# Heads 16 to 31 first in the recurrent-memory step, and the tail projections dealt to four places

## The chip, the core and the metric

The kernel runs on one core of one Trainium2 chip. The metric is the device time in microseconds of one execution; the lower, the better. In the profile the engines are PE (TensorE, matmuls), PEld (its weight loads), DVE (VectorE), ACT (ScalarE), POOL (GpSimd) and SP (SyncE, which issues most DMAs).

## The reference

Four layers in a row, A B A B, on 2048 tokens of 640 channels in bfloat16, each added to its input. Layer A is a segmented attention with a compressive memory (32 heads of 20), and the change doesn't touch it. Layer B carries eight memory tokens through 64 segments of 32 tokens, with 32 heads of 128:

```python
for s in range(n_seg):                      # 64, one after the other
    h = concatenate([mem, xs], axis=1)      # 8 memory tokens, 32 tokens
    q, k, v = h @ Wq, h @ Wk, h @ Wv        # 32 heads of 128 each
    scores = q k^T * scale                  # 40 x 40 a head
    p = softmax(where(mask, scores, -1e9))
    o = (p v) @ Wo
    mem = o[:, :M]                          # the next segment's memory
    outs.append(o[:, M:])
```

The order of the steps is forced: segment s+1 needs the memory that segment s wrote.

## The kernel before

`layer_B` (a loop over `s` from line 914 on) does one segment per step. Two things are worked ahead so that a step has only what depends on the memory. The first is the **tails**: the last 8 tokens of each segment are projected for eight segments at once. `tail_unit(T, k, ...)` (line 757) makes one of eight units of the q and k tails: 8 heads by 5 chunks of 128 channels, 40 matmuls of 64 columns into the PSUM tile `b_tail`; `tail_evac` (772) copies it to `b_tu` and stores that to the DRAM tensor `QKd`; `tails_load` brings a segment's part back as `b_tl`, and POOL copies it into `KT` and `QZ`. `vtail_unit` and `vtail_evac` do the same for v. Each step does one unit of the following group of segments. The second is the state of a step: the projections in step `s` (`b_Ka`, `b_Qa`, `b_Kb`, `b_Qb`, `b_Va`, `b_Vb`; a is heads 0 to 15, b heads 16 to 31) are of the 8 memory tokens of segment s and of 24 tokens of segment s+1, 32 columns together. So half of a transposed tile goes to this step's `KT[s]`, `QT[s]` (the DVE `scatter`), and the other to the next step's (`x_scatter` on ACT).

Each projection (`thin_mm`, 714) is 5 chunks of four matmuls, each on 32 columns of the array (rows say 128x512). `kq` (932) scales and casts the result to `b_kq`; `transp4` turns it with four 128x128 transposes (`b_TPak` and so on). The scores live in PSUM tiles called `b_SP`, which start from a mask (`mask_mm`, a 128x128 matmul with the identity). There are 12 groups of 40 columns: groups 0 to 3 hold the tails' scores (`QZ`), 4 to 7 those of heads 0 to 15, 8 to 11 those of heads 16 to 31. Before, groups 0 to 7 share one tile and 8 to 11 have another. Then follow `soft_max`, `soft_sub`, `soft_exp`, `soft_sum`, the reciprocal and `soft_p`, which writes `b_Px` (DVE) and `b_Pm` (POOL); the transposed probabilities `b_PTP`, copied to `b_PTa` and `b_PTb`; the products with v (`pv`, tiles `b_OTP`, copied to `b_OTsb`); the output projection (`b_OPS`, and `b_OPSd` for the deferred rows); the next memory (`b_msb`, `b_MT`, copied into `b_HX`); and `x_out`, two adds on DVE.

On PE, ACT, DVE and POOL the order within a step is exactly the order in which the code is written: every call goes through `_OrdEng` (87), which ties each instruction to the one before it on its engine. SP is not tied (line 28). Small PSUM tiles come in turn from five buffers (`ps_tile`, 629); `b_tail`, `b_OPS` and `b_OPSd` have one each, and `b_TPbq` used that of `b_tail`.

The part of the step that the change rearranges is written like this before:

```python
Ka; ka = kq(Ka, "act");  Qa; qa = kq(Qa, "dve")      # 1005 on
Kb; kb = kq(Kb, "act");  Qb; qb = kq(Qb, "act")
TPak, scatter, x_scatter; TPaq, ...; TPbk, ...
SPa = mask_mm(0); TPbq, ...; SPb = mask_mm(1)
scores((SPa, SPb))                 # a, tails, b
softmax of both, Px, Pm;  Va;  Vb
tail_unit(.., 0, 6)                # 30 matmuls
p_transp(0); p_transp(1)
tail_unit(.., 6, 8); tail_evac     # 10 matmuls
```

Of the kernel before, what the change touches and what calls it, by code (L numbers as in the profile page):

```python
# [18 lines left out]
F32 = mybir.dt.float32  # L19
BF16 = mybir.dt.bfloat16  # L20
ACT = mybir.ActivationFunctionType
ALU = mybir.AluOpType
AX = mybir.AxisListType
# [6 lines left out]
NCH = 5  # L30
# [568 lines left out]
def layer_B(nc, tc, C, W, x_src, xb_src, x_dst, mem0, B_Wv, B_Wo, nsteps=64, out_bf16=False, tag=""):  # L599
    SCB = 1.0 / math.sqrt(128.0)  # L600
    nc_raw = nc
    nc = _OrdNC(tc, nc_raw, engines=ORDER_ENGINES)
    NG = nsteps // 4
    NT = nsteps // 8
    QKd = tc.dram_tile([nsteps, 128, 512], BF16, name=f"b_QKd{tag}")
    VTd = tc.dram_tile([nsteps, 8, 4096], BF16, name=f"b_VTd{tag}")
    with ExitStack() as ctx:
# [21 lines left out]
        def ps_tile(shape, dtype, name):  # L629
            return pp.tile(shape, dtype, name=name, tag="ps")  # L630
# [80 lines left out]
                return HXz[:, :, 0, :]  # L711
            return HX[u // 4][:, :, u % 4, :]

        def thin_mm(cols_ap, Wt, b, name):
            ps = ps_tile([128, 512], F32, name)
            for c in range(NCH):
                for j in range(4):
                    n = 4 * b + j
                    nc.tensor.matmul(ps[32 * j:32 * j + 32, :], lhsT=cols_ap[:, c, :], rhs=Wt[:, c, 512 * n:512 * n + 512],
                                     start=(c == 0), stop=(c == NCH - 1), tile_position=(0, 32 * j), skip_group_check=True)  # L720
            return ps

        def transp4(sb, name, tp=None):
            if tp is None:
                tp = ps_tile([128, 4, 128], BF16, name)
            for i in range(4):
                nc.tensor.transpose(tp[:, i, :], sb[:, 128 * i:128 * i + 128], C.identb[:])
            return tp

        def scatter(eng, tp, b, dst_t, t0, t1, c0):  # L730
            src = tp[:].rearrange("p i (j t) -> p i j t", j=4)[:, :, :, t0:t1]
            dst = dst_t[:, 16 * b:16 * b + 16, c0:c0 + (t1 - t0)].rearrange("p (j i) c -> p i j c", j=4)
            evac(eng, dst, src)
# [20 lines left out]

        tail_ps = {}

        def tail_unit(T, k, i0, i1, shared=False):
            proj, hg = divmod(k, 4)
            Wt = W.wk if proj else W.wq
            if i0 == 0:  # L760
                if shared:
                    tail_ps[0] = ps_tile([128, 8, 64], F32, "b_tail")
                else:
                    tail_ps[0] = po.tile([128, 8, 64], F32, name="b_tail", tag="tail")
            ps = tail_ps[0]
            for i in range(i0, i1):
                h = 8 * hg + i
                for c in range(NCH):
                    nc.tensor.matmul(ps[:, i, :], lhsT=Wt[:, c, 128 * h:128 * h + 128], rhs=TX[T][:, c, :, :].rearrange("p s t -> p (s t)"),
                                     start=(c == 0), stop=(c == NCH - 1))  # L770

        def tail_evac(T, k, eng, home=None):
            proj, hg = divmod(k, 4)
# [52 lines left out]
            for c in range(NCH):  # L826
                nc.sync.dma_start(HX[0][:, c, 1, 0:8], mem0[:, 128 * c:128 * c + 128].rearrange("t p -> p t"))
        for k in range(8):
            tail_unit(0, k, 0, 8, shared=True)
            tail_evac(0, k, "act" if k % 2 == 0 else "dve", (kqp, "kq"))  # L830
            if k % 4 == 1 and 2 + k // 4 < n0:
                ln_norm(2 + k // 4)
            if k % 4 == 3 and 2 + k // 4 < n0:
                ln_spread(ln_ready.pop(0))
# [21 lines left out]
            evac("act" if b == 0 else "dve", Vth[:, b, :], ps[:])  # L856
        vtails_in(0)
        if NT > 1:
            tail_unit(1, 0, 0, 8, shared=True)
            tail_evac(1, 0, "act")  # L860
            vtail_evac(1, 0, vtail_unit(1, 0), "dve")

# [51 lines left out]
        for s in range(nsteps):  # L914
# [13 lines left out]
            def x_scatter(tp, b, D_):  # L928
                if not last:
                    scatter("act", tp, b, D_[s + 1], 8, 32, 8 if D_ is KT else 0)  # L930

            def kq(ps, eng, scale=None):
                sb = kqp.tile([128, 512], BF16, name="b_kq", tag="kq")
                evac(eng, sb[:], ps[:], scale)
                return sb

            GR = ((0, 8), (8, 12))

            def mask_mm(a):
                g0, g1 = GR[a]  # L940
                SP = ps_tile([128, g1 - g0, 40], F32, f"b_SP{a}")
                nc.tensor.matmul(SP[:].rearrange("p g k -> p (g k)"), lhsT=C.identb[:], rhs=mask12[:, g0:g1, :].rearrange("p g k -> p (g k)"),
                                 start=True, stop=False, skip_group_check=True)
                return SP

            def scores(SPs):
                for b in range(2):
                    for j in range(4):
                        for i in range(4):
                            h = 16 * b + 4 * j + i  # L950
                            nc.tensor.matmul(SPs[b][32 * i:32 * i + 32, j + 4 * (1 - b), :], lhsT=QT[s][:, h, :], rhs=KT[s][:, h, :],
                                             start=False, stop=True, tile_position=(0, 32 * i), skip_group_check=True)
                    if b == 0:
                        qz = QZ[s % 2][:].rearrange("p x c -> p (x c)")
                        for j in range(4):
                            for e in range(2):
                                for t4 in range(4):
                                    pr = 8 * (t4 // 2) + 2 * j + t4 % 2
                                    nc.tensor.matmul(SPs[0][32 * t4:32 * t4 + 16, j, :], lhsT=qz[:, 24 * pr + 8 * e:24 * pr + 8 * e + 16],
                                                     rhs=KT[s][:, 2 * pr + e, :],  # L960
                                                     start=False, stop=True, tile_position=(0, 32 * t4), skip_group_check=True)

            negmax = sm.tile([128, 12], F32, name="b_negmax", tag="negmax")
            ssum = sm.tile([128, 12], F32, name="b_ssum", tag="ssum")
            rs = sm.tile([128, 12], F32, name="b_rs", tag="rs")
            E_ = wk.tile([128, 12, 40], BF16, name="b_E", tag="E0")

            def soft_max(a, SP):
                nc.vector.tensor_reduce(out=negmax[:, slice(*GR[a])], in_=SP[:], axis=AX.X, op=ALU.max, negate=True)

            def soft_sub(a, SP):
                n_ = GR[a][1] - GR[a][0]
                nc.vector.tensor_tensor(out=SP[:], in0=SP[:], in1=negmax[:, slice(*GR[a])].unsqueeze(2).to_broadcast([128, n_, 40]), op=ALU.add)

            def soft_exp(a, SP):
                nc.scalar.activation(out=E_[:, slice(*GR[a]), :], in_=SP[:], func=ACT.Exp)

            def soft_sum(a):
                nc.vector.tensor_reduce(out=ssum[:, slice(*GR[a])], in_=E_[:, slice(*GR[a]), :], axis=AX.X, op=ALU.add)

            def soft_p(eng, P_, k0, k1, g0, g1):
                eng.tensor_tensor(out=P_[:, g0:g1, 0:k1 - k0], in0=E_[:, g0:g1, k0:k1],
# [19 lines left out]
                                             tile_position=(32 * j, 0), skip_group_check=True)  # L1002


            Ka = thin_mm(cols, W.wk, 0, "b_Ka")
            ka = kq(Ka, "act")
            Qa = thin_mm(cols, W.wq, 0, "b_Qa")
            qa = kq(Qa, "dve", SCB)
            Kb = thin_mm(cols, W.wk, 1, "b_Kb")
            kb = kq(Kb, "act")  # L1010
            Qb = thin_mm(cols, W.wq, 1, "b_Qb")
            qb = kq(Qb, "act", SCB)

            TPak = transp4(ka, "b_TPak")
            scatter("dve", TPak, 0, KT[s], 0, 8, 32)
            x_scatter(TPak, 0, KT)
            TPaq = transp4(qa, "b_TPaq")
            scatter("dve", TPaq, 0, QT[s], 0, 8, 24)
            x_scatter(TPaq, 0, QT)
            TPbk = transp4(kb, "b_TPbk")  # L1020
            scatter("dve", TPbk, 1, KT[s], 0, 8, 32)
            x_scatter(TPbk, 1, KT)
            SPa = mask_mm(0)
            TPbq = transp4(qb, "b_TPbq", po.tile([128, 4, 128], BF16, name="b_TPbq", tag="tail"))
            scatter("dve", TPbq, 1, QT[s], 0, 8, 24)
            x_scatter(TPbq, 1, QT)
            SPb = mask_mm(1)
            scores((SPa, SPb))
            soft_max(0, SPa)
            soft_max(1, SPb)  # L1030
            soft_sub(0, SPa)
            soft_exp(0, SPa)
            soft_sub(1, SPb)
            soft_exp(1, SPb)
            soft_sum(0)
            soft_sum(1)
            nc.vector.reciprocal(out=rs[:], in_=ssum[:])
            soft_p(nc.vector, Px, 0, 32, 0, 8)
            soft_p(nc.gpsimd, Pm, 32, 40, 0, 12)
# [9 lines left out]
            if ln_ready:  # L1049
                ln_spread(ln_ready.pop(0))  # L1050
            if work:
                tail_unit(work[0], work[1], 0, 6)
            ptpa = p_transp(0)
            PTa = wk.tile([128, 2, 4, 40], BF16, name="b_PTa", tag="PTa")
            ptpb = p_transp(1)
# [2 lines left out]
                for pt, ptp, eng in ((PTa, ptpa, "act"), (PTb, ptpb, "dve")):  # L1058
                    evac(eng, pt[:, :, 2 * hf:2 * hf + 2, :], ptp[:, :, 2 * hf:2 * hf + 2, :])
            if work:  # L1060
                tail_unit(work[0], work[1], 6, 8)
            if unit:
                tail_evac(unit[0], unit[1], "act")
            otf = [ps_tile([128, 2, 4, 40] if j else [128, 4, 40], F32, "b_OTP") for j in range(4)]
            ots = {j: (otf[j][:, 0, :, :], otf[j][:, 1, :, :]) for j in (1, 2, 3)}
# [25 lines left out]
            def vtail_some(n_):  # L1091
                nonlocal vps, vc
                if work and vc < NCH:
                    vps = vtail_unit(work[0], work[1], vc, min(NCH, vc + n_), vps)
                    vc = min(NCH, vc + n_)

            vtail_some(2)
            if not last:
# [5 lines left out]
                for pi, (ca, cb) in enumerate(parts):  # L1104
# [6 lines left out]
                    nc.vector.tensor_copy(dst[:, ca:cb, 0:8], mt[:])  # L1111
                    vtail_some((1, 1, NCH)[pi])
            vtail_some(NCH)
            if unit:
                vtail_evac(unit[0], unit[1], vps, "act")
            if od and od["n"] == 4:
# [111 lines left out]
```

## Time and profile before

| | |
|---|---|
| median of 3 runs | 2793.08 us (2786.16 to 2794.82) |
| the profiled execution's own time | 2787.25 us |
| its span, first to last instruction | 2785.5 us |
| mean granted clock of PE | 0.981 |
| PE busy | 2574.7 us, 92% |
| DVE, ACT, POOL busy | 1686.6, 1584.9, 715.2 us |
| steps of layer B, start to start | 126, sum 1890.7 us, median 14.88 us |

A line of the timeline gives the start in us from the beginning of the span, the duration, the engine, the source line, the operation, what it writes and reads, and how many were merged; in brackets the idle time of the engine before it and what ended that. Nearly all instructions of layer B carry line L101, that of the helper which keeps the order, so they are told apart by their tiles. Matmuls overlap: the duration of a group holds the time in which the last result runs out, and what a group costs PE is the distance from its start to the start of the next. A row of the stretches gives the length, the busy time of PE, PEld, DVE, ACT and POOL with their instructions in brackets, and then the granted clock, the share of the DMA engines and the GB/s.

### The profile page before, as it was taken

The page shows a single profiled execution, that of the slowest core. Times are in us where ns is not written, and L with a number is a line of the kernel's source. Part 1 is how long each engine was busy: PE and PEld are TensorE (multiplying, and loading weights), DVE is VectorE, ACT ScalarE, POOL GpSimd, SP SyncE. Part 2 cuts the span into 40 slices and gives each one's busy share as a digit, 9 for nine tenths or more (in the row PEclk, how much of TensorE's full clock was granted, in tenths as well). Part 3 has the DMA queues.
Part 4 walks back from the last instruction along what each step waited for, and adds up shares of the span by engine and source line. Part 5 has one row for each costly group of instructions (what it writes and reads, how often), then busy time and mean ns, then how long its engine had stood idle before and what let it go on. Part 6 is the DMA issues. An engine that isn't in the chain of part 4 may idle for free. (4 is left out here: it accounts for less than half of the span.)

```text
span 2785.5 us, 146956 instructions
## 1 busy us (share of the span) xinstructions
PE 2574.7 (92%) x65414; PEld 1700.1 (61%) x65480; DVE 1686.6 (61%) x4553; ACT 1584.9 (57%) x3708; POOL 715.2 (26%) x1645
## 2 busy tenths in 40 slices
PE   5888879999999999999978888799999999999998
PEld 3555556666666666666645555556666666666665
DVE  6888854555555555555578888445555555555554
ACT  4888854555555555544458888445555455555443
POOL 4666541111111111111146665411111111111110
PEclk9999979999999999999989999899999999999999
DMA  6111162221212212111120111721211121211110
GB/s 239 41 44 40 30 195 69 45 46 41 45 43 45 43 43 45 43 39 30 41 99 28 51 49 37 231 47 39 42 42 40 40 44 40 43 41 38 39 26 20
DMA packets 322300, 156.36 MB, mean 56 GB/s; under 512 B 245760, under 2 KB 310400, under 8 KB 318592
## 3 DMA queue, kind: packets, MB, share of 16 engines
q1 hardware_dynamic: 320224, 136.47, 19.2%
q8 instruction: 512, 8.39, 1.3%
q10 hardware_dynamic: 1440, 10.49, 1.0%
q14 instruction: 124, 1.02, 0.1%
HBM read 95.15 MB, written 51.71 MB: 53 GB/s over the span
## 5 line engine op out<-in xcount | busy, mean ns | idle before, releaser
L101 PEld LDWEIGHTS <-b_HX 128*32 128x32 bf16 x15360 | 430.2, 97 | 341.0 <-issue 14.1
L101 POOL TENSOR_TENSOR b_Pm<-b_E,b_rs 128x96 bf16<-128x96 bf16 x128 | 63.3, 495 | 1443.2 <-ACT b_Vth L101 1094.2
L400 DVE TENSOR_REDUCE a_nm<-a_S 128x2 f32<-128x1024 f32 (+3 forms) x512 | 396.5, 815 | 51.4 <-PE a_T L101 26.6
L442 ACT ACTIVATE a_PT<-a_T 128x1024 bf16<-128x1024 f32 (+1 forms) x384 | 325.4, 889 | 84.9 <-PE a_T L101 50.6
L101 PE MATMUL b_OPS<-b_wo,b_OTsb 128*32 128x320 bf16 x8192 | 308.0, 301 | 10.3 <-issue 8.5
L101 PEld LDWEIGHTS <-b_OTsb 128*32 128x32 bf16 x8192 | 200.5, 97 | 97.0 <-DVE b_OTsb L101 24.1
L101 DVE CAST b_HX<-b_MT 128x8 bf16<-128x8 f32 x372 | 63.7, 172 | 277.5 <-PE b_MT L101 272.2
L444 POOL TENSOR_SCALAR_AFFINE_SELECT a_PT<-a_PT 128x256 bf16<-128x256 bf16 (+1 forms) x384 | 193.5, 520 | 143.2 <-ACT a_PT L442 141.0
L101 ACT CAST b_msb<-b_OPS 128x64 bf16<-128x64 f32 x378 | 69.3, 256 | 237.7 <-PE b_OPS L101 237.7
L101 ACT CAST b_kq<-b_Kb 128x512 bf16<-128x512 f32 x128 | 74.9, 585 | 201.6 <-PE b_Kb L101 201.6
L101 DVE COPY b_KT<-b_TPak 128x128 bf16<-128x128 bf16 x128 | 28.8, 225 | 227.0 <-PE b_TPak L101 227.0
L101 PE MATMUL b_Va<-b_wv,b_HX 128*32 128x512 bf16 x2520 | 160.8, 380 | 0.0
L101 PE MATMUL b_Vb<-b_wv,b_HX 128*32 128x512 bf16 x2520 | 160.1, 379 | 0.0
L101 PEld LDWEIGHTS <-b_kq 128*128 128x128 bf16 x2080 | 116.8, 98 | 68.8 <-ACT b_kq L101 55.6
L101 PE MATMUL b_Ka<-b_wk,b_HX 128*32 128x512 bf16 x2520 | 158.8, 379 | 0.0
L101 DVE TENSOR_SCALAR b_kq<-b_Qa 128x512 bf16<-128x512 f32 x128 | 88.5, 691 | 115.9 <-PE b_Qa L101 112.9
L101 PE MATMUL b_Kb<-b_wk,b_HX 128*32 128x512 bf16 x2520 | 158.6, 379 | 0.0
L101 PE MATMUL b_Qb<-b_wq,b_HX 128*32 128x512 bf16 x2520 | 158.6, 379 | 0.0
L101 PE MATMUL b_Qa<-b_wq,b_HX 128*32 128x512 bf16 x2520 | 158.6, 379 | 0.0
L101 DVE CAST b_OTsb<-b_OTP 128x160 bf16<-128x160 f32 (+1 forms) x384 | 122.3, 374 | 39.6 <-PE b_OTP L101 39.6
L101 PE MATMUL b_vtail<-b_wv,b_TX 128*32 128x256 bf16 x2880 | 137.7, 271 | 6.6 <-issue 3.5
L101 ACT ACTIVATE b_E<-b_SP 128x320 bf16<-128x320 f32 (+1 forms) x256 | 81.1, 368 | 109.0 <-PE b_Va L101 95.3
(195 smaller groups left out, 5764.8 us busy)
## 6 DMA issues: line engine op xcount, KB each, us to landing
b_QKd<-b_tu SPq DMA_DIRECT2D x128, 128.0 KB
b_tl<-b_QKd SPq DMA_DIRECT2D x128, 128.0 KB
b_wv<-in_B_Wv_dram SPq DMA_DIRECT2D x10, 1024.0 KB
b_wo<-in_B_Wo_dram SPq DMA_DIRECT2D x16, 640.0 KB
b_VTd<-b_vt SPq DMA_DIRECT2D x256, 32.0 KB
b_Vth<-b_VTd SPq DMA_DIRECT2D x512, 16.0 KB
b_XO<-xres SPq DMA_DIRECT2D x256, 30.0 KB
b_wk<-in_B_Wk_dram ACTq DMA_DIRECT2D x5, 1024.0 KB
```

The costliest lines, as they stand in the source:

```text
L101: r = f(*a, **k)
L400: nc.vector.tensor_reduce(out=nm[:, qc, 2 * pr:2 * pr + 2], in_=X[:, :, o:o + w_], axis=AX.X, op=ALU.max, negate=True)
L442: nc.scalar.activation(out=PT[:, :, b:b + width], in_=Y[:, :, 0:width], func=ACT.Exp, scale=SC)
L444: nc.gpsimd.affine_select(out=dv, in_=dv, pattern=[[0, 2], [0, diag], [1, 128]], compare_op=ALU.is_ge, fill=0.0, base=0, channel_multiplie ...
```

## The change

The two head halves change places: `b_Qb`, `b_Kb` and `b_Ka` are projected first, heads 16 to 31 are transposed, masked, scored and taken through max and subtraction while `b_Qa` is still being projected (two of its five chunks come before these scores, three after). The evacuation of `b_Qb` moves from ACT to DVE and that of `b_Qa` from DVE to ACT. The tails' scores get a PSUM tile of their own, so there are three masks of 160 columns, and three of each softmax instruction. `b_TPbq` moves to the five shared buffers. The tail unit, which was cut by heads into 30 and 10 matmuls, is cut by matmuls at 5, 8 and 20: five ahead of `b_TPaq`, three after `b_Vb`, twelve after `b_PTP`, and twenty at the end of the step, with its evacuation behind them. The core of the diff:

```diff
+    TCUT = (5, 8, 20)
...
-            GR = ((0, 8), (8, 12))
+            GR = ((0, 4), (4, 8), (8, 12))
...
-            Ka = thin_mm(cols, W.wk, 0, "b_Ka")
-            ka = kq(Ka, "act")
-            Qa = thin_mm(cols, W.wq, 0, "b_Qa")
-            qa = kq(Qa, "dve", SCB)
-            Kb = thin_mm(cols, W.wk, 1, "b_Kb")
-            kb = kq(Kb, "act")
-            Qb = thin_mm(cols, W.wq, 1, "b_Qb")
-            qb = kq(Qb, "act", SCB)
+            Qb = thin_mm(cols, W.wq, 1, "b_Qb")
+            qb = kq(Qb, "dve", SCB)
+            Kb = thin_mm(cols, W.wk, 1, "b_Kb")
+            kb = kq(Kb, "act")
+            Ka = thin_mm(cols, W.wk, 0, "b_Ka")
+            ka = kq(Ka, "act")
+            TPbq = transp4(qb, "b_TPbq")
+            scatter("dve", TPbq, 1, QT[s], 0, 8, 24)
+            x_scatter(TPbq, 1, QT)
+            TPbk = transp4(kb, "b_TPbk")
+            scatter("dve", TPbk, 1, KT[s], 0, 8, 32)
+            x_scatter(TPbk, 1, KT)
+            SPb = mask_mm(2)
+            Qa = thin_mm(cols, W.wq, 0, "b_Qa", 0, 2)
+            scores(1, SPb)
+            soft_max(8, 12, SPb[:])
+            soft_sub(8, 12, SPb[:])
+            thin_mm(cols, W.wq, 0, "b_Qa", 2, NCH, Qa)
+            qa = kq(Qa, "act", SCB)
             TPak = transp4(ka, "b_TPak")
             scatter("dve", TPak, 0, KT[s], 0, 8, 32)
+            SPt = mask_mm(0)
+            if work:
+                tail_unit(work[0], work[1], 0, TCUT[0])
+            soft_exp(8, 12, SPb[:])
             x_scatter(TPak, 0, KT)
             TPaq = transp4(qa, "b_TPaq")
             scatter("dve", TPaq, 0, QT[s], 0, 8, 24)
             x_scatter(TPaq, 0, QT)
...
+            SPa = mask_mm(1)
+            tail_scores(SPt)
+            scores(0, SPa)
+            soft_max(0, 4, SPt[:])
+            soft_sub(0, 4, SPt[:])
+            soft_exp(0, 4, SPt[:])
+            soft_max(4, 8, SPa[:])
+            soft_sub(4, 8, SPa[:])
+            soft_exp(4, 8, SPa[:])
+            soft_sum(8, 12)
+            soft_sum(0, 4)
+            soft_sum(4, 8)
...
-                tail_unit(work[0], work[1], 0, 6)
+                tail_unit(work[0], work[1], TCUT[0], TCUT[1])
...
-                tail_unit(work[0], work[1], 6, 8)
-            if unit:
+                tail_unit(work[0], work[1], TCUT[1], TCUT[2])
+            if unit and TCUT[2] == 40:
                 tail_evac(unit[0], unit[1], "act")
...
             vtail_some(NCH)
+            if work and TCUT[2] < 40:
+                tail_unit(work[0], work[1], TCUT[2], 40)
+            if unit and TCUT[2] < 40:
+                tail_evac(unit[0], unit[1], "act")
             if unit:
                 vtail_evac(unit[0], unit[1], vps, "act")
```

More of the change, by code (lines that the diff above doesn't have):

```diff
@@ L712, in cols_of, with thin_mm @@
             return HX[u // 4][:, :, u % 4, :]
-        def thin_mm(cols_ap, Wt, b, name):
-            ps = ps_tile([128, 512], F32, name)
-            for c in range(NCH):
+        def thin_mm(cols_ap, Wt, b, name, c0=0, c1=NCH, ps=None):
+            if ps is None:
+                ps = ps_tile([128, 512], F32, name)
+            for c in range(c0, c1):
                 for j in range(4):
@@ L755, in layer_B, with tail_unit @@
         tail_ps = {}
-        def tail_unit(T, k, i0, i1, shared=False):
+        def tail_unit(T, k, n0, n1, shared=False):
             proj, hg = divmod(k, 4)
             Wt = W.wk if proj else W.wq
-            if i0 == 0:
+            if n0 == 0:
                 if shared:
@@ L765, in tail_unit @@
             ps = tail_ps[0]
-            for i in range(i0, i1):
+            for n_ in range(n0, n1):
+                i, c = divmod(n_, NCH)
                 h = 8 * hg + i
-                for c in range(NCH):
-                    nc.tensor.matmul(ps[:, i, :], lhsT=Wt[:, c, 128 * h:128 * h + 128], rhs=TX[T][:, c, :, :].rearrange("p s t -> p (s t)"),
-                                     start=(c == 0), stop=(c == NCH - 1))
+                nc.tensor.matmul(ps[:, i, :], lhsT=Wt[:, c, 128 * h:128 * h + 128], rhs=TX[T][:, c, :, :].rearrange("p s t -> p (s t)"),
+                                 start=(c == 0), stop=(c == NCH - 1), skip_group_check=True)
         def tail_evac(T, k, eng, home=None):
@@ L828, in layer_B @@
         for k in range(8):
-            tail_unit(0, k, 0, 8, shared=True)
+            tail_unit(0, k, 0, 40, shared=True)
             tail_evac(0, k, "act" if k % 2 == 0 else "dve", (kqp, "kq"))
@@ L858, in layer_B @@
         if NT > 1:
-            tail_unit(1, 0, 0, 8, shared=True)
+            tail_unit(1, 0, 0, 40, shared=True)
             tail_evac(1, 0, "act")
@@ L944, in mask_mm, with scores, tail_scores @@
                 return SP
[L946 to L961, printed above, removed]
+            def scores(b, SP):
+                for j in range(4):
+                    for i in range(4):
+                        h = 16 * b + 4 * j + i
+                        nc.tensor.matmul(SP[32 * i:32 * i + 32, j, :], lhsT=QT[s][:, h, :], rhs=KT[s][:, h, :],
+                                         start=False, stop=True, tile_position=(0, 32 * i), skip_group_check=True)
+            def tail_scores(SP):
+                qz = QZ[s % 2][:].rearrange("p x c -> p (x c)")
+                for j in range(4):
+                    for e in range(2):
+                        for t4 in range(4):
+                            pr = 8 * (t4 // 2) + 2 * j + t4 % 2
+                            nc.tensor.matmul(SP[32 * t4:32 * t4 + 16, j, :], lhsT=qz[:, 24 * pr + 8 * e:24 * pr + 8 * e + 16],
+                                             rhs=KT[s][:, 2 * pr + e, :],
+                                             start=False, stop=True, tile_position=(0, 32 * t4), skip_group_check=True)
             negmax = sm.tile([128, 12], F32, name="b_negmax", tag="negmax")
@@ L966, in layer_B, with soft_max, soft_sub, soft_exp @@
             E_ = wk.tile([128, 12, 40], BF16, name="b_E", tag="E0")
[L968 to L979, printed above, removed]
+            def soft_max(g0, g1, SP):
+                nc.vector.tensor_reduce(out=negmax[:, g0:g1], in_=SP, axis=AX.X, op=ALU.max, negate=True)
+            def soft_sub(g0, g1, SP):
+                nc.vector.tensor_tensor(out=SP, in0=SP, in1=negmax[:, g0:g1].unsqueeze(2).to_broadcast([128, g1 - g0, 40]), op=ALU.add)
+            def soft_exp(g0, g1, SP):
+                nc.scalar.activation(out=E_[:, g0:g1, :], in_=SP, func=ACT.Exp)
+            def soft_sum(g0, g1):
+                nc.vector.tensor_reduce(out=ssum[:, g0:g1], in_=E_[:, g0:g1, :], axis=AX.X, op=ALU.add)
             def soft_p(eng, P_, k0, k1, g0, g1):
@@ L1019, in layer_B @@
             x_scatter(TPaq, 0, QT)
[L1020 to L1036, printed above, removed]
+            SPa = mask_mm(1)
[10 more added lines that the diff above has]
+            soft_sum(4, 8)
             nc.vector.reciprocal(out=rs[:], in_=ssum[:])
```

## Prediction

> **What bounds the kernel now.** I read the page first (busy shares), then the waits, then the timeline of single B steps, then the stretches by stage.
>
> ```profile
> PE 2574.7 (92%) x65414; PEld 1700.1 (61%) x65480; DVE 1686.6 (61%) x4553; ACT 1584.9 (57%) x3708; POOL 715.2 (26%) x1645
> ```
>
> TensorE (PE) is busy for 92% of the span, no other engine for more than 61%. The change touches only the 2 x 64 steps of layer B. The starts of the first `b_Ka` matmuls give 126 step lengths: fastest 14.67 us apart from the first of each layer, median 14.88, mean 15.01, 1890.7 in all. One step without pauses, from the timeline (start, duration, engine; 792.74 to 807.41, so 14.67 us):
>
> ```profile
> 795.97 1.25 PE L101 MATMUL b_Qb<-b_wq,b_HX 128*32 128x512 bf16 x20
> ...
> 797.15 0.40 PE L101 MATMUL b_TPak<-c_identb,b_kq 128*128 128x128 bf16 x4
> 797.34 0.60 ACT L101 ACTIVATE b_kq<-b_Qb 128x512 bf16<-128x512 f32 x1 [0.50 <-PE b_Qb L101]
> ...
> 797.99 0.40 PE L101 MATMUL b_TPbq<-c_identb,b_kq 128*128 128x128 bf16 x4
> ...
> 798.22 0.23 PE L101 MATMUL b_SP<-b_mask,c_identb 128*128 128x160 bf16 x1
> ...
> 798.38 0.28 PE L101 MATMUL b_SP<-b_KT,b_QT 128*32 128x40 bf16 x16
> 798.42 0.23 DVE L101 COPY b_QT<-b_TPbq 128x128 bf16<-128x128 bf16 x1 [0.16 <-PE b_TPbq L101]
> 798.50 0.41 PE L101 MATMUL b_SP<-b_KT,b_QZ 128*16 128x40 bf16 x32
> ...
> 798.74 0.32 PE L101 MATMUL b_SP<-b_KT,b_QT 128*32 128x40 bf16 x16
> 798.87 1.28 PE L101 MATMUL b_Va<-b_wv,b_HX 128*32 128x512 bf16 x20
> ...
> 799.01 0.72 DVE L101 TENSOR_REDUCE b_negmax<-b_SP 128x8 f32<-128x320 f32 x2 [0.36 <-PE b_SP L101]
> 799.65 0.72 DVE L101 TENSOR_TENSOR b_SP<-b_SP,b_negmax 128x320 f32<-128x320 f32 x2
> 799.96 1.27 PE L101 MATMUL b_Vb<-b_wv,b_HX 128*32 128x512 bf16 x20
> 800.25 0.63 ACT L101 ACTIVATE b_E<-b_SP 128x320 bf16<-128x320 f32 x2 [0.78 <-PE b_Va L101]
> 800.72 0.71 DVE L101 TENSOR_REDUCE b_ssum<-b_E 128x8 f32<-128x320 bf16 x2 [0.35 <-ACT b_E L101]
> ...
> 801.16 1.05 PE L101 MATMUL b_tail<-b_TX,b_wq 128*128 128x64 bf16 x30
> ...
> 801.47 0.23 DVE L101 RECIPROCAL b_rs<-b_ssum 128x12 f32<-128x12 f32 x1
> 801.73 0.78 DVE L101 TENSOR_TENSOR b_Px<-b_E,b_rs 128x256 bf16<-128x256 bf16 x2
> ...
> 802.22 0.24 PE L101 MATMUL b_PTP<-c_identb,b_Px 128*128 128x128 bf16 x2
> ...
> 802.75 0.45 PE L101 MATMUL b_tail<-b_TX,b_wq 128*128 128x64 bf16 x10
> ...
> 803.13 0.52 PE L101 MATMUL b_OTP<-b_PTa,b_Vth 32*128 32x40 bf16 x32
> ```
>
> PE runs group after group, in program order. A projection of 20 matmuls starts every 1.08 us, five rounds of 0.216. Single starts in the trace put the 64-column tail matmuls 0.029 apart. So the only real hole is before `b_PTP`: 30 tails need 0.87, but 802.22 - 801.16 is 1.06, hence 0.19 of waiting for `b_Px`; the eight `b_PTP` matmuls take 0.53, against 0.42 in steps where the layer-norm transposes fill that hole, hence 0.11 more. **0.30 us a step, 38 us in all, is the most that an earlier softmax can win**, besides the pauses of PE at "issue" (15.01 - 14.67, see the rivals).
>
> **The change, part by part** (per step, us).
>
> *What stays equal.* Six projections, 16 transposes, 64 score matmuls, 40 tail matmuls: the same number. Masks: 320 + 160 columns become 3 x 160, the same 480 columns. One evacuation moves from ACT to DVE (`b_Qb`, 0.69 there by the `b_Qa` row) and one from DVE to ACT (`b_Qa`, 0.60). DVE does `b_Qb` after the `x_out` adds (793.98 to 794.99 in this step), so by about 2.9 us into the step, and `b_TPbq` wants it only at 3.34: hidden. The DMAs are the same; only the store of `b_tu` goes to the step's end, with `tail_evac` (0.60, ACT) ahead of `vtail_evac` (0.37). On ACT both end about 1.3 us into the next step, and ACT's next work there (`b_Kb`) comes at 2.44: hidden. On SP the store now stands before the next `b_tl` load, which is issued only some 10.7 us into the step after the POOL copies free the tile: hidden too. Without that cover, a store and a load would have to land first, some 4 us once in eight steps (an estimate from 2 us each): 0.5 a step.
>
> *Changes of array shape: +0.40.* From the 128x32 form to 128x128, `b_Qb` takes 1.18 until `b_TPak` starts instead of 1.08: 0.10. From 128x128 to 128x32, the mask of 160 columns takes 0.16 until the scores start; 160 columns at 512 per 0.216 are 0.07: 0.09. Ten tails before `b_OTP` take 0.38 instead of 0.29: 0.09 again. The new order adds two pairs: mask to `b_Qa`, `b_Qa` to `b_TPak`; `b_vtail` to the last 20 tails, those to the next `b_Qb`. 2 x (0.10 + 0.09), with the first matmul of a group some 0.01 longer: 0.40. All on PE's path. Bounds 0.30 to 0.45.
>
> *A new wait before `b_TPaq`: +0.37.* `b_Qa` is now projected just before its transposes. In the rows, `b_Qb` streams until 795.97 + 1.08 = 797.05; ACT starts at 797.34 (0.29 later), takes 0.60, and `b_TPbq` starts 0.05 after its end: 0.93 from the end of the stream. Until now a mask and 12 transposes covered that. Now PE has the shape change 0.10, `b_TPak` 0.24, a mask 0.07, five tails 0.15: 0.56. The remaining 0.37 is a wait, and everything on PE is queued behind it: matmuls run in program order, so no later tail can fill it. Bounds 0.30 and 0.50 (ACT also holds two `x_scatter` copies ahead, 2 x 0.5, over by 5.1 us; `b_Qa` ends at 5.2).
>
> *A wait before the scores of heads 0 to 15: +0.10.* From `b_TPbq` to DVE's scatter are 0.43, the scatter 0.23, and 0.05 to 0.10 back to PE: 0.71 to 0.76. PE has `b_TPaq` 0.23, mask with shape change 0.16, 32 tail scores 0.24: 0.63. I take 0.10; bounds 0 and 0.20.
>
> *The softmax hole: 0.19 becomes 0.46, +0.27.* Heads 16 to 31 are early now, and their max, subtraction and exponential hide under the rest of `b_Qa` and the transposes. The remaining chain, counted from the start of `b_Va`: the tails' scores end 0.13 earlier, DVE follows 0.27 behind (798.74 to 799.01), so the tails' max starts at about 0.04. The 160-column forms last 0.315 (max), 0.323 (subtraction), 0.298 (exponential), 0.309 (sum) in the groups by form. A dependent DVE instruction starts 0.035 after its source ends (sum to reciprocal), an independent one may start 0.085 before the last one's end (492 + 315 ns show as 0.72). Max 0.04 to 0.36, subtraction 0.39 to 0.71, second max 0.63 to 0.94, second subtraction 0.98 to 1.30; ACT 0.115 later (in the 126 steps) 1.42 to 1.71; sum 1.74 to 2.05; reciprocal 2.09 to 2.32; `b_Px` of eight groups (0.425) 2.35 to 2.78; `b_PTP` 0.06 later, **2.84**, against 3.35 before (798.87 to 802.22). So the chain is 0.5 shorter; but its cover falls further. Before: 1.09 + 1.20 + 0.87 = 3.16. Now only three tails stand behind `b_Vb`: 1.09 + 1.20 + 0.09 = **2.38**. Wait 2.84 - 2.38 = 0.46. Its second part (0.11, second `b_Px` and POOL's `b_Pm`) stays. Bounds 0.25 and 0.75. What is late next, `b_PTa` on ACT, is now covered by 12 tails instead of 10. In the 24 steps with layer-norm transposes more of these (0.29 of PE) falls into the hole, but their copies (0.57 and 0.32 on ACT) push `b_PTa` back by about as much: no term.
>
> *The tails themselves: 0.* The 27 taken from the softmax hole reappear as 5, 2 and 20 elsewhere; the 20 at the end of the step fill nothing, since `b_Ka` after `b_vtail` shows no gap (807.31 to 807.41).
>
> Sum: 0.40 + 0.37 + 0.10 + 0.27 = **+1.14 a step**, 126 steps 144 us, the last step of each layer about 1 more: 145. Against the profiled execution (2787.25): 2932. The median of the runs is 5.8 above it (2793.08): **2938**.
>
> *A rule weighed.* The granted clock in the stretch 700 to 1000 (B) is 1.00 while PE is 98% busy; in 1390 to 1830 (mostly layer A) PE is 81% busy and the clock 0.94. My step would be about 93% busy with holes under 0.5 us.
>
> ```profile
> 700.00:1000.00 300.00, 295.19 (x8665) 195.21 (x8661) 164.55 (x514) 156.04 (x409) 37.47 (x104) 1.00 0.20 43
> 1390.00:1830.00 440.00, 356.68 (x5451) 235.28 (x5484) 330.20 (x668) 310.09 (x590) 239.12 (x488) 0.94 0.26 83
> ```
>
> The Trainium skill ("TensorE: Matmul & The Clock Gate", the section on the HAM clock gate) lets the clock fall only after an idle window of about 3.4 us, by which nothing is added to the sum. The same page ("A second HAM failure mode: psum-queue depth-cycling") says that frequent micro-idles between matmul groups can make the clock oscillate; by that the time would be the clock rival's below.
>
> **Rivals.**
> 1. *Pauses swallow part.* PE loses 0.33 a step at "issue" (mean against fastest), most around `b_OPS`. If its instructions catch up during the new waits, up to 42 us return: 2896. Against: the pauses lie after the waits, 1 to 4 us later. 12%.
> 2. *Longer hops.* Every new wait rests on hops between engines, and DVE and ACT queues are fuller. 0.25 more a step: 2970. 12%.
> 3. *The clock falls* to layer A's 0.94: 14.4 us of streaming x 0.064 = 0.92 a step, 116 us on top: 3054. Against: B at 1.00 with a hole of 0.3 in every step. 4%.
> 4. *Faster: instruction supply is the real bound.* Place: PE's issue pauses. If all vanish (-0.33) and the old hole (-0.30) too, the step is 14.67 - 0.30 + 0.40 plus the new waits; it beats 15.01 as long as these stay under 0.24. I find 0.94 (0.37 + 0.10 + 0.46). With none: 30 us less, 2763. 3%, and 2% for ending about even.
> 5. *It doesn't do what it says*: the built program's PE order shows `b_Qb`, `b_Kb`, `b_Ka` first and the tails at 5, 3, 12, 20. None.
>
> **Numbers.** My case 67%. The range 2894 to 2974 holds it with the bounds of its waits, rivals 1 and 2. 0.3% (8 us) is what a measurement of this kernel can tell from no change. Slower 95%, same 2%, faster 3%.
>
> **What would show it.** Right: a B step of about 15.8 us without pauses; holes before `b_TPaq` (released by ACT `b_kq`) and before `b_PTP` (by DVE `b_Px`) of 0.4 to 0.5 each; `b_Qa`'s last 12 matmuls to `b_TPak` 0.75; 20 tails at the step's end 0.8 with both shape changes. Wrong: no hole at `b_TPaq`, `b_PTP` following `b_Vb` within 0.3, or a step under 15.2.

## The result and the profile after

The changed kernel takes 2947.11 us (median of 4 runs, 2941.18 to 2955.25) against 2789.62 (2785.36 to 2794.82) of the kernel before on the same chip: 1.0566 times as long (95% interval 1.0532 to 1.0600). The profiled execution lasted 2948.28 with a span of 2946.5, 161.0 longer than before. The 126 steps of layer B, read as before from one first projection matmul to the next, sum to 2047.1 (mean 16.25), 156.4 more; so nearly all of the loss lies in the steps. A step without pauses (the shortest that recurs, the first step of each layer left out) takes 15.92, 1.245 more.

The page's first part of the changed kernel:

```profile
PE 2655.4 (90%) x65608; PEld 1664.2 (56%) x65608; DVE 1755.1 (60%) x4937; ACT 1617.2 (55%) x3836; POOL 715.1 (24%) x1645
```

PE still carries the time, at a slightly smaller share. The timeline of one step of the changed kernel without pauses (777.83 to 793.75; start, duration, engine, tiles, in brackets the idle time before):

```profile
782.35 0.82 PE L101 MATMUL b_Qa<-b_wq,b_HX 128*32 128x512 bf16 x12
782.60 0.33 DVE L101 TENSOR_REDUCE b_negmax<-b_SP 128x4 f32<-128x160 f32 x1 [0.54 <-PE b_SP L101]
782.96 0.33 DVE L101 TENSOR_TENSOR b_SP<-b_SP,b_negmax 128x160 f32<-128x160 f32 x1
...
783.10 0.40 PE L101 MATMUL b_TPak<-c_identb,b_kq 128*128 128x128 bf16 x4
...
783.28 0.60 ACT L101 ACTIVATE b_kq<-b_Qa 128x512 bf16<-128x512 f32 x1 [0.54 <-PE b_Qa L101]
783.33 0.23 PE L101 MATMUL b_SP<-b_mask,c_identb 128*128 128x160 bf16 x1
...
783.40 0.31 PE L101 MATMUL b_tail<-b_TX,b_wk 128*128 128x64 bf16 x5
...
783.93 0.40 PE L101 MATMUL b_TPaq<-c_identb,b_kq 128*128 128x128 bf16 x4 [0.22 <-ACT b_kq L101]
...
784.76 1.25 PE L101 MATMUL b_Va<-b_wv,b_HX 128*32 128x512 bf16 x20
784.81 0.33 DVE L101 TENSOR_REDUCE b_negmax<-b_SP 128x4 f32<-128x160 f32 x1 [0.22 <-PE b_SP L101]
785.24 0.33 DVE L101 TENSOR_TENSOR b_SP<-b_SP,b_negmax 128x160 f32<-128x160 f32 x1
785.48 0.31 DVE L101 TENSOR_REDUCE b_negmax<-b_SP 128x4 f32<-128x160 f32 x1
...
785.90 0.33 DVE L101 TENSOR_TENSOR b_SP<-b_SP,b_negmax 128x160 f32<-128x160 f32 x1
786.14 0.84 DVE L101 TENSOR_REDUCE b_ssum<-b_E 128x4 f32<-128x160 bf16 x3
...
787.01 0.23 DVE L101 RECIPROCAL b_rs<-b_ssum 128x12 f32<-128x12 f32 x1
787.02 0.26 PE L101 MATMUL b_tail<-b_TX,b_wk 128*128 128x64 bf16 x3
...
787.28 0.78 DVE L101 TENSOR_TENSOR b_Px<-b_E,b_rs 128x256 bf16<-128x256 bf16 x2
...
787.76 0.24 PE L101 MATMUL b_PTP<-c_identb,b_Px 128*128 128x128 bf16 x2 [0.48 <-ACT b_Vth L101]
...
793.06 0.76 PE L101 MATMUL b_tail<-b_TX,b_wk 128*128 128x64 bf16 x20
...
793.75 0.40 PE L101 MATMUL b_Qb<-b_wq,b_HX 128*32 128x512 bf16 x4
```

Read the starts, not the durations. Five tails start at 783.40 and need 5 x 0.029 = 0.15, but `b_TPaq` starts 0.53 later. The bracket says only 0.22 idle, because the last tail's result still runs out; the place in PE's stream that stood empty is 0.38. In the same way three tails (0.09) start at 787.02 and `b_PTP` at 787.76, 0.74 later: 0.65 empty, against 0.19 before. And the 20 tails at the end take 0.69 in full view.

PE's rows of the waits in the changed kernel (total us, times, longest):

```profile
PE b_PTP L101 <- ACT b_Vth L101: 43.9, 102, 0.5
PE b_TPaq L101 <- ACT b_kq L101: 28.6, 128, 0.5
...
PE b_PTP L101 <- DVE b_Px L101: 15.3, 26, 0.8
...
PE b_OTP L101 <- DVE b_PTb L101: 5.1, 20, 0.3
...
PE b_OTP L101 <- DMA b_xt<-xres_bf: 1.0, 4, 0.3
```

Before, the only one of these rows was `b_PTP` on `b_Px`, with 3.2 us in 7 waits. The first row names the wrong releaser: `b_Vth` only happens to end just before `b_PTP` starts (787.73 here). In max_max_sub_sub below, `b_PTP` starts at 9.54 us into the step while that copy runs until 9.89 (medians of 126 steps), so it doesn't wait for it. It is `b_Px`: its first part ends 0.056 to 0.058 before `b_PTP` in every step of the kernel before, of the changed one and of max_max_sub_sub. The last row names a wrong releaser too; the part on the layer-norm steps below comes back to it.

The stretch 700 to 1000 of the changed kernel (length; busy PE, PEld, DVE, ACT, POOL; granted clock; DMA share; GB/s):

```profile
700.00:1000.00 300.00, 283.97 (x8029) 175.35 (x8022) 161.71 (x530) 150.15 (x399) 34.80 (x98) 1.00 0.19 40
```

PE is busy for 95% of it instead of 98%, at the same clock of 1.00.

### The profile page after: what moved, and what is told of

The parts are those of the page before. It is cut to its first block, busy times and chain, and to the rows that moved or that the text cites. A ratio compares the mean times of both kernels' runs of the same rounds, so it can differ in the third digit from the quotient of the medians.

```text
span 2946.5 us, 147885 instructions
## 1 busy us (share of the span) xinstructions
PE 2655.4 (90%) x65608; PEld 1664.2 (56%) x65608; DVE 1755.1 (60%) x4937; ACT 1617.2 (55%) x3836; POOL 715.1 (24%) x1645
## 4 chain that ended last, share of the span: by engine, by line
PE 52%; ACT 9%; DVE 5%; issue 2%; DMA 2%; POOL 1%; SPq 0%; ACTq 0%; DVEq 0%; POOLq 0%
PE b_OPS L101 8%; PE b_Qa L101 4%; PE b_Qb L101 4%; PE b_Kb L101 4%; PE b_Ka L101 4%; PE b_tail L101 3%; PE b_Vb L101 3%; PE b_Va L101 3%; ACT a_PT L442 3%; PE b_SP L101 3%; PE b_OTP L101 2%; PE b_PTP L101 2%; PE b_OPSd L101 2%; ACT b_kq L101 2%; PE b_vtail L101 2%
## 5 line engine op out<-in xcount | busy, mean ns | idle before, releaser
L101 PEld LDWEIGHTS <-b_HX 128*32 128x32 bf16 x15360 | 366.4, 96 | 341.5 <-issue 14.7
L101 ACT ACTIVATE b_E<-b_SP 128x160 bf16<-128x160 f32 x384 | 116.0, 302 | 123.6 <-DVE b_SP L101 120.2
L101 DVE TENSOR_REDUCE b_negmax<-b_SP 128x4 f32<-128x160 f32 x384 | 123.6, 322 | 99.3 <-PE b_SP L101 99.2
L101 PE MATMUL b_Qa<-b_wq,b_HX 128*32 128x512 bf16 x2520 | 171.7, 380 | 0.0
L101 ACT CAST b_OTsb<-b_OTP 128x320 bf16<-128x320 f32 x256 | 96.5, 429 | 118.7 <-PE b_OTP L101 118.7
L101 DVE COPY b_QT<-b_TPbq 128x128 bf16<-128x128 bf16 x128 | 28.8, 225 | 220.4 <-PE b_TPbq L101 220.4
```

What stands on the lines that cost most here:

```text
L101: r = f(*a, **k)
```

## The experiments

Theory: four terms add up (array shapes; the wait before `b_TPaq`; the wait before the scores of heads 0 to 15; a softmax whose cover fell further than its chain). Rivals: the order of the heads alone, or the dealing of the tails alone, makes the whole loss; or longer hops between engines in general; or PE's pauses at issue, or the softmax's extra instructions. "Step" is a step without pauses: 14.675 before, 15.92 after. Ratios are to the kernel before in the runs of the same chip (medians 2777.77 for the first four kernels, 2783.03 for the last four), so kernels are compared by ratio and step, not by time.

**The order alone (order_only).** The changed kernel with the tails where they were, 30 and 10. The tails' own score tile, the exchanged evacuations and the new place of `b_TPbq` stay in it:

```diff
-    TCUT = (5, 8, 20)
+    TCUT = (0, 30, 40)
```

> The changed kernel with the tails back at their old places (30 behind b_Vb, 10 behind b_PTP, none elsewhere): the new order alone. Waits-and-shapes theory: the pause-free step of 15.92 us has 1.21 of waits in it (0.37 before b_TPaq, 0.08 before the scores of heads 0 to 15, 0.65 and 0.11 at b_PTP), 14.71 without them; two shape changes less give 14.50; the wait before b_TPaq grows to 0.53 without its five tails, the one before b_PTP goes (chain 3.00, cover 3.13). Step 15.1 to 15.2, about 2857 us. Rival, PE's pauses at issue set the loss: no part of the 157 us comes back, since the number of instructions is the same, about 2945. Rival, the softmax's extra instructions cost the time: no gain either, the softmax is unchanged here.

2841.02 (2838.64 to 2842.56), ratio 1.0225 (1.0205 to 1.0244), step 15.13. Its waits:

```profile
PE b_TPaq L101 <- ACT b_kq L101: 46.6, 128, 0.4
...
PE b_PTP L101 <- DVE b_Px L101: 1.2, 2, 0.6
```

`b_PTP` no longer waits, the wait before `b_TPaq` is deeper without the five tails (0.53 by starts). Up to `b_Va` the step grew by 0.77; from `b_Va` to `b_PTP`, the eight `b_PTP` included, it shrank by 0.34. More than half of the loss is gone with the softmax and the work unchanged, so neither PE's pauses nor the extra softmax instructions make the whole of it.

**The tails alone (tails_only).** The order before, with the tail unit at 5, 8 and 20 (five ahead of `b_TPaq` there too), and `b_TPbq` in the shared buffers so that `b_tail` can stay open:

```diff
+    TCUT = (5, 8, 20)
...
-            TPbq = transp4(qb, "b_TPbq", po.tile([128, 4, 128], BF16, name="b_TPbq", tag="tail"))
+            TPbq = transp4(qb, "b_TPbq")
...
```

> The kernel before with only the tails dealt to four places (5 before b_TPaq, 3 behind b_Vb, 12 behind b_PTP, 20 at the end; b_TPbq in the shared buffers, so that b_tail can stay open): the dealing alone. Waits-and-shapes theory: the old chain of 3.35 us keeps its length but its cover falls from 3.16 to 2.37, so the wait before b_PTP grows by 0.8; two shape changes add 0.21; the mask for heads 16 to 31 waits some 0.1 for a buffer. Step 15.7 to 15.8 against 14.67, about 2925 us. Rival, the order of the heads is what costs: close to 2795.

2916.96 (2912.22 to 2921.19), ratio 1.0498 (1.0475 to 1.0521), step 15.63, a little under the 15.7 expected.

```profile
PE b_PTP L101 <- DVE b_Px L101: 100.4, 128, 1.1
```

From the start of `b_Va` to that of `b_PTP` are 3.34, as before: with 30 tails in between or with three, the softmax chain sets it, and taking 27 tails out left 0.96 of emptiness (1.05 for three tails that need 0.09). The step grows by 0.96, nearly all of it what those tails cost elsewhere: 5 x 0.029, 20 x 0.029, and 0.21 of array shapes at the end of the step, 0.94 together. So each half of the change loses by itself (0.45 and 0.96 a step), and neither makes the whole 1.245; nor do the two add up to it, since both act on the same waits.

**The tails in the new holes (tails_in_holes).**

```diff
-    TCUT = (5, 8, 20)
+    TCUT = (17, 28, 40)
```

> The changed kernel with the tails cut at 17, 28 and 40: 17 before b_TPaq, 11 behind b_Vb, 12 behind b_PTP, none at the end. Waits-and-shapes theory: twelve more tails fill 0.35 of the 0.37 before b_TPaq, eight more take 0.23 of the 0.65 before b_PTP, and the two shape changes at the end go (0.21): step 15.92 - 0.79 = 15.13, about 2848 us. Rival, the wait before b_TPaq is something other than the evacuation of b_Qa and moves with the tails: step 15.5, about 2895. Rival, pauses: 2945.

2834.51 (2831.95 to 2843.47), ratio 1.0208 (1.0182 to 1.0233), step 15.12.

```profile
PE b_PTP L101 <- ACT b_Vth L101: 19.8, 81, 0.3
...
PE b_PTP L101 <- DVE b_Px L101: 9.2, 24, 0.8
...
PE b_TPaq L101 <- ACT b_kq L101: 0.7, 2, 0.4
```

Seventeen tails ahead of `b_TPaq` take the 0.53 that five and a wait took, and eight more ahead of `b_PTP` its 0.74. So both emptinesses are waits, of the sizes read above. The step falls by 0.80: 20 x 0.029 and the array shapes (0.2) of the tails at the end.

**The softmax in pairs (max_max_sub_sub).** Both max first, then both subtractions, as in the order before:

```diff
             soft_max(0, 4, SPt[:])
+            soft_max(4, 8, SPa[:])
             soft_sub(0, 4, SPt[:])
             soft_exp(0, 4, SPt[:])
-            soft_max(4, 8, SPa[:])
             soft_sub(4, 8, SPa[:])
```

> The changed kernel with one line moved: both maxes (tails, heads 0 to 15) before both subtractions, so that no subtraction stands right behind the max that it needs. If the chain on DVE sets the wait before b_PTP: the subtraction of the second tile ends 0.39 us earlier (the two 0.10 gaps behind the maxes and the order), the wait falls from 0.65 to 0.26, step 15.53, about 2898 us. Rival, POOL's b_Pm or ACT's queue ends that wait: under 10 us of gain, about 2940.

2893.07 (2887.95 to 2902.96), ratio 1.0419 (1.0386 to 1.0453), step 15.52.

```profile
PE b_TPaq L101 <- ACT b_kq L101: 28.6, 128, 0.5
...
PE b_PTP L101 <- DVE b_Px L101: 4.4, 17, 0.4
```

From `b_Va` to `b_PTP` are now 2.61 instead of 3.00, and the step gains all of that; the wait before `b_TPaq` hasn't moved. So the place of one DVE instruction made 0.39 of the step's 1.245, about a third (by the ratios, 1.0566 and 1.0419, about a quarter of the kernel's loss).

**No tails at the end (tails_mid).**

```diff
-    TCUT = (5, 8, 20)
+    TCUT = (5, 8, 40)
```

> The changed kernel with the last 20 tails moved from the step's end to behind b_PTP (cut at 5, 8 and 40): it takes away two shape changes and leaves the waits before b_TPaq and b_PTP as they are. If a shape change costs what the rows say: 0.21 a step, and up to 0.2 more because the waits inside b_OTP for b_PTa and b_PTb are then covered: step 15.5 to 15.7, 2895 to 2921 us. Rival, a shape change costs nothing and the rows show only a modelled end: 2945.

2892.0 (2888.9 to 2894.39), ratio 1.0388 (1.0373 to 1.0403), step 15.62. The same tails, on the path in both places, cost 0.30 less behind `b_PTP`: the array shapes at the step's end (some 0.21) and 0.08 before `b_OPSd`, since `b_OTP` takes 0.62 instead of 0.70.

**`b_Qa` projected early (qa_early).** Its 20 matmuls come before `b_TPbq`, so that other work stands between it and its transposes:

```diff
+            Qa = thin_mm(cols, W.wq, 0, "b_Qa")
+            qa = kq(Qa, "act", SCB)
             TPbq = transp4(qb, "b_TPbq")
...
-            Qa = thin_mm(cols, W.wq, 0, "b_Qa", 0, 2)
...
-            thin_mm(cols, W.wq, 0, "b_Qa", 2, NCH, Qa)
-            qa = kq(Qa, "act", SCB)
```

> The changed kernel with b_Qa projected whole before b_TPbq, not split around the scores of heads 16 to 31: undoes the late b_Qa. Waits-and-shapes theory: the wait of 0.37 before b_TPaq goes, but the scores of heads 16 to 31 then stand right behind b_TPbk and wait about 0.3 for DVE's scatter, and the scatters of heads 0 to 15 queue behind a max and a subtraction on DVE: the loss moves, step 15.8 to 16.0, 2935 to 2960 us. Rival, the late b_Qa is the heart of the loss: step 15.55, about 2900.

2963.22 (2956.64 to 2965.92), ratio 1.0641 (1.0624 to 1.0659), step 16.08: slower than the change, and above what either theory expected.

```profile
PE b_PTP L101 <- DVE b_Px L101: 67.4, 128, 0.9
PE b_SP L101 <- DVE b_KT L101: 55.3, 255, 0.5
```

The wait before `b_TPaq` is gone, but the split of `b_Qa` was cover, too: without it each set of scores waits for its scatter. From a mask to its scores are 0.48 and 0.41, of which 0.16 is the mask with its shape change: 0.32 and 0.25 of waiting, where the change waits 0.38 before `b_TPaq` and 0.08 before scores. Up to `b_Va` the step grew by 0.08, and `b_PTP` follows `b_Va` by 3.09 instead of 3.00: together the 0.16 of the step.

**Both mends together (mended).** The order of the change, softmax in pairs, the tails in the holes:

```diff
-    TCUT = (5, 8, 20)
+    TCUT = (17, 29, 40)
...
             soft_max(0, 4, SPt[:])
+            soft_max(4, 8, SPa[:])
...
-            soft_max(4, 8, SPa[:])
```

> The changed kernel with both mends: maxes before subtractions, and the tails cut at 17, 29 and 40 (12 behind b_Vb, 11 behind b_PTP, none at the end). Waits-and-shapes theory: what stays against the kernel before is two shape changes (0.20), 0.08 before the scores of heads 0 to 15 and 0.1 at b_PTP, less the old hole: step 14.75 to 14.85, about 2803 us, close to the kernel before and not below it. If the account lacks a term, the step stays over 15.2.

2792.86 (2786.23 to 2797.48), ratio 1.0031 (1.0018 to 1.0045), step 14.72, a little under the 14.75 expected.

```profile
PE b_TPaq L101 <- ACT b_kq L101: 0.7, 2, 0.4
PE b_PTP L101 <- DVE b_Px L101: 0.7, 2, 0.4
```

With both holes filled, the new order of the heads is back within 0.3% of the kernel before and no better. Up to `b_Va` the step is 0.28 longer than before, its 17 tails not counted: array shapes, 0.08 before the scores, the rest of the wait before `b_TPaq`. Behind that it wins 0.24: the 0.19 before `b_PTP` and some small things. The other part of the old hole stays, for the eight `b_PTP` still take 0.52 (0.53 before).

**The tails' own score tile alone (own_tile_ops).** The kernel before, with only its scores divided: the tails' in a tile of their own (in the buffer of `b_OPS`, free then), scored first, and three max, three subtractions with their exponentials, three sums:

```diff
-            GR = ((0, 8), (8, 12))
+            GR = ((0, 4), (4, 8), (8, 12))
...
+                    SP = po.tile([128, g1 - g0, 40], F32, name="b_SP0", tag="ops")
...
+            SPt = mask_mm(0)
+            SPa = mask_mm(1)
...
+            SPs = (SPt, SPa, SPb)
+            scores(SPs)
+            for a in range(3):
+                soft_max(a, SPs[a])
+            for a in range(3):
+                soft_sub(a, SPs[a])
+                soft_exp(a, SPs[a])
+            for a in range(3):
+                soft_sum(a)
```

> The kernel before with one part of the change alone: the tails' scores in a PSUM tile of their own (in the buffer that b_OPS leaves free at that time of the step), tails scored first, three maxes, three subtractions, three exponentials, three sums; order of the heads and places of the tails as before. Waits-and-shapes theory: the tails' max starts 0.25 us earlier and the chain from the scores to b_Px shortens from 3.35 to about 3.05, below its cover of 3.16: the hole of 0.30 closes in the 102 steps without layer-norm transposes, no new shape change: step 14.40, about 2760 us, below both kernels. Rival, more DVE instructions lengthen the chain: 2790 to 2800.

2759.96 (2757.33 to 2764.11), ratio 0.9916 (0.9903 to 0.9930): 0.8% faster than the kernel before, and so faster than both, step 14.39. Its timeline in one such step:

```profile
924.67 0.79 DVE L101 TENSOR_REDUCE b_negmax<-b_SP 128x4 f32<-128x160 f32 x3 [0.22 <-PE b_SP L101]
924.69 1.28 PE L101 MATMUL b_Va<-b_wv,b_HX 128*32 128x512 bf16 x20
...
925.37 0.78 DVE L101 TENSOR_TENSOR b_SP<-b_SP,b_negmax 128x160 f32<-128x160 f32 x3
...
926.15 0.77 DVE L101 TENSOR_REDUCE b_ssum<-b_E 128x4 f32<-128x160 bf16 x3
...
926.98 1.05 PE L101 MATMUL b_tail<-b_TX,b_wq 128*128 128x64 bf16 x30
...
927.86 0.23 PE L101 MATMUL b_PTP<-c_identb,b_Px 128*128 128x128 bf16 x2
```

Thirty tails from 926.98 to 927.86 take 0.88 for their 0.87: no hole. The eight `b_PTP` take 0.37 instead of 0.53. That is the 0.30 that the prediction named as the most that an earlier softmax can win, and the step wins 0.285. The chain starts earlier: the first max comes 0.02 ahead of `b_Va` (924.67 to 924.69), where it came 0.14 behind it before, and `b_PTP` follows `b_Va` by 3.17 instead of 3.34. In the layer-norm steps, whose transposes filled the old hole, there was nothing to win: 14.67 against 14.68.

## Why the prediction was right

The forecast was 2938, within 2894 to 2974; 2947 came. By its own steps, per step:

| step of the prediction | forecast | measured |
|---|---|---|
| changes of array shape | +0.40 | +0.41 |
| wait before `b_TPaq` | +0.37 | +0.38 |
| wait before the scores of heads 0 to 15 | +0.10 | +0.08 |
| softmax hole 0.19 to | 0.46 (+0.27) | 0.65 (+0.46) |
| not in the sum: `b_OTP` | 0 | -0.06 |
| sum; step without pauses | +1.14 | +1.27; +1.245 |

**Array shapes.** By starts: `b_Qb` until `b_Kb` 1.09 (1.08 before), `b_Ka` until `b_TPbq` 1.185, a mask of 160 columns until a 128x32 group 0.16 and until the 128x128 tails 0.07, the last 12 `b_Qa` 0.75 for three rounds of 0.216, the last four `b_vtail` 0.21 for 0.11, the 20 tails 0.69 for 0.58. The Trainium skill ("TensorEngine Tiling (Array Packing)", Key Properties) says that a change of the tiling mode drains TensorE, without a figure; the rows here agree and put it at 0.09 to 0.10 in each direction. tails_mid, which drops one pair, confirms it.

**The softmax hole is the mis-sized term.** The chain was put at 2.84 from the start of `b_Va` and took 3.00; the cover was put at 2.38 and was 2.35. The step that failed is the chain's: it let each subtraction start 0.035 after its max, the distance from sum to reciprocal (786.98 to 787.01 in the lines above). But these two subtractions start 0.104 after their max in the median of 126 steps: 785.14 to 785.24, and 785.79 to 785.90. Two of these on the chain are 0.14, the max itself (0.325) the rest. max_max_sub_sub takes both distances out and lets the instructions overlap: 2.61.

The distance isn't that of a max and its subtraction as such. In the same kernel the subtraction of heads 16 to 31 stands right behind its max too and starts 0.034 after it (782.60 + 0.325 = 782.93 to 782.96 above). The trace holds the difference: the two late subtractions wait for a semaphore of ACT besides DVE's own, and one of the two waits is an instruction by itself (EVENT_SEMAPHORE), which stands between max and subtraction; the early one waits for DVE alone and has no such instruction. In qa_early the subtraction of heads 16 to 31 has it as well, and there it starts after 0.104. Over all kernels here, every subtraction right behind its max comes after 0.034 to 0.035 without it, and after 0.103 or more with it.

**"No term" for the layer-norm steps was wrong,** by about 8 us: the fastest of these 24 steps takes 16.26, 0.34 more than 15.92; before, 14.68 against 14.675. The prediction looked at `b_PTa`, which ends as in the other steps (10.96 into the step). What stops PE is the fourth `b_OTP` matmul, 0.44 behind the third:

```profile
804.40 0.56 DVE L101 CAST b_PTb<-b_PTP 128x160 bf16<-128x160 f32 x2 [0.42 <-PE b_PTP L101]
...
804.65 0.20 PE L101 MATMUL b_OTP<-b_PTa,b_Vth 32*128 32x40 bf16 x3
...
805.10 0.35 PE L101 MATMUL b_OTP<-b_PTa,b_Vth 32*128 32x40 bf16 x29 [0.25 <-DVE b_PTb L101]
```

The waits name `b_PTb` for 20 of the 24 steps and a DMA for 4. It is `b_PTb` in all: there this matmul waits for DVE's semaphore, and it starts 0.145 to 0.147 after the second copy of `b_PTb` ends, in the changed kernel, in tails_only, in qa_early and in max_max_sub_sub, although that copy ends at 11.20, 10.91, 11.37 and 10.81 us into the step. In the other kernels' layer-norm steps no matmul before the 30th waits for DVE: in tails_in_holes the copy ends as late (11.19), and the fourth matmul has started 0.19 before. The four kernels with the wait are those with 20 tails and `tail_evac` at the step's end; why it stands at the fourth matmul there, no run settles. In max_max_sub_sub such a step loses as much (15.87 against 15.52), but most of it ahead of `b_OTP`, because `b_PTa`, behind the layer-norm copies on ACT, ends later (its first half at 10.75 instead of 10.37).

**The total.** 126 x 1.245 = 157, and the steps grew by 156.4 in all: what the layer-norm steps added (8), shorter pauses gave back (8). Neither was in the sum, and that they cancel is luck. Another 4.6 (161.0 - 156.4) lie outside these steps, where 1 was forecast.

**The rivals.** *Pauses swallow part:* in the 102 steps without layer norm, the mean lies 0.33 above the step without pauses before and 0.25 after; with the other 24, about 8 of the 42 us came back in these two profiles, not more. *Longer hops:* not in general, since the waits at `b_TPaq` and the scores came out as forecast; two hops within DVE were longer, by 0.07 each. *The clock falls:* it stayed at 1.00 with gaps of 0.08 to 0.65 in every step. The rule of the Trainium skill on the idle window ("TensorE: Matmul & The Clock Gate", the section on the HAM clock gate) agrees with this row; the oscillation by micro-idles, which the same page tells of, is not seen in any of these kernels: in the stretch 700 to 1000 each of them has 0.99 or 1.00. *Faster, by instruction supply:* it needed new waits under 0.24 and met 0.38 + 0.08 + 0.65. Still, own_tile_ops shows where the gain was: the old hole could be won, by 0.285 of 0.30, without a new order.

## What to carry to other kernels

Work that fills a wait is worth its own length only as long as it is there: count for each wait the chain and the cover after the change, since here the chain became 0.34 shorter and its cover 0.81. A group that is split or dealt out pays about 0.2 us for each extra pair of array shapes on TensorE. And when a change has several parts, try each alone: the one that shortened the chain and kept its cover won 0.8%, the order (with that part still in it) cost 2.3% and the tails alone 5.0%. Before a distance between two instructions is carried from one pair to another, look at what each of them waits for: here 0.035 went with one wait and 0.104 with two.

## What the runs showed of the hardware

A DVE instruction that needs the result of the one just before it starts 0.034 to 0.035 us after that ends (reciprocal after sum, product after reciprocal, subtraction after max), but 0.104 after where it waits for a second engine too, with one of the two waits as an instruction of its own between them; an independent instruction starts 0.085 before the last one's end. So max, subtraction, max, subtraction lasts 0.39 longer than max, max, subtraction, subtraction (8.40 against 8.01 us into the step). On PE, the fourth `b_OTP` matmul of the layer-norm steps, which has such a wait ahead of it, starts 0.145 after the copy that it waits for, while `b_PTP` starts 0.057 after `b_Px`. And the releaser that a wait row names can be one that merely ended last: `b_Vth` was named for 102 of the 128 waits of `b_PTP`, which max_max_sub_sub shows not to depend on it, and a DMA for 4 of the 24 waits of `b_OTP` for `b_PTb`.
